# Casts tied to the first output block of tile b - 3, and transposed loads ahead of row transposes

## The chip, the cores and the metric

One core of a Trainium2 chip. The metric is the device time of one execution in microseconds (us). The kernel before takes 305.76 us, median of 3 runs (305.43 to 306.01). An execution counts as slow when it takes over 1.5% longer than the fastest of its kernel.

## The reference

Attention over 8 batches of 8 heads, 576 tokens, 64 features each, with two banded masks, followed by a two-layer network with a gate:

```python
scores = where(mask, q @ k.T / 8, -1e9)      # heads 0-3: the last 32 tokens; 4-7: every 4th of the last 128
attn   = softmax(scores) @ v
x      = attn.transpose(0, 2, 1, 3).reshape(4608, 512)
h      = x @ w_in                            # 512 -> 2048
out    = (h * sigmoid(beta * h)) @ w_out     # 2048 -> 512
```

Inputs and the output are fp32; the kernel computes in bf16 with fp32 accumulation.

## The kernel before

The 4608 tokens make 8 batches (b, 576 tokens) for the attention and 9 tiles (t, 512 tokens) for the network. Both run interleaved: while TensorE works on tile t, it also does the attention of batch b = t + 1. A small list scheduler in the kernel, the planner, decides before launch in which order every engine gets its instructions. It uses estimated durations (for a DMA, `dma` is its time in the queue and `lat` its time to land) and priorities `vt`. The planner decides **order only**. At run time the waits follow from what each instruction reads and writes.

For b >= 3 the way from inputs to the network is this. GpSimd (POOL) issues **casts**: q and k from fp32 to bf16 scratch in DRAM, v into SBUF. SyncE (SP) issues **transposed loads** dk, dq, kT, qT from the scratch. Then come the attention, the **rows** x<-xsp and x<-xdm (results to DRAM), and the **row transpose** xT<-x that brings them back transposed, for the first product of tile b - 1, b and b + 1. SyncE issues all its transfers in one order: one that must wait holds up those behind it, as dk behind xT at 95 us in the trace before (the prediction shows the lines). A small POOL copy, **pace**, stands ahead of the casts and holds them back.

```python
# the row transpose (L502 of the profile) and the rows in front of it
rows = dram_pool.tile([S // 2, HD], BF16, name=f"x{b}_{j}")
out = [plan.op([("SP", 500)], ...dma_start(out=rows[...], in_=xsp[j]...),           # L475
               [vdone[0, j], vdone[1, j]], vt_of[f"X1{j}"], dma=1200, lat=2000)]
...
o = plan.op([("SP", 1300)], lambda e: nc.sync.dma_start_transpose(out=cols, in_=rows[:]), out + dil,
            vt_of[f"X1{j}"], dma=1500, lat=3500)                                     # L502
...
def spread(e):                                       # vd<-st, L232: on POOL or VectorE, as the planner finds it
    copy(e, vd[kv][:, :, :, 0:D], vd16_of[b])
o = plan.op([("POOL", 1100), ("DVE", 620)], spread, ...)
...
def slot_h(t, fb, c0, n, vt, apart):                 # first product (L811), tanh on ACT (L820), gate on VectorE (L825)
    ...
def block_cols(t, tb, vts, lo, hi, last_one):        # second product of 128 tokens (L846), then its evacuation (result to SBUF):
    ...
    ev = plan.op([act(hi - lo), dve(hi - lo)], evac, [prev] + w, vts[3] - .01, group=g)   # osb<-bank, L861
...
def loads(b):                                        # called after tile t = b - 1 has been put on the list
    ...
    mid = (b - 2) * S + S // 2
    def t_pace(e, b=b, mid=mid):
        nc.gpsimd.tensor_copy(out=pace[:], in_=(
            xT[0:1, 0, mid - 1:mid + 1] if b - 2 >= BY_DMA else g_t[b % 2][0:1, 0, 0:2]))
    go = plan.op([("POOL", 150)], t_pace, behind + (...), b - 2.4)
    for n, (z, h0) in enumerate(((0, 4), (1, 4), (0, 0), (1, 0))):
        c = cast(b, z, h0, [go], b - 2 + .01 * n)    # L384
        ld[b]["x", z, h0] = crossbar(b, z, h0, [c] + war(*key), b - 2 + .01 * n)     # L438
```

So in the kernel before, the casts of b wait until xT of b - 2 has landed.

The softmax here doesn't subtract the row's maximum and nothing guards it: scores larger than these inputs give would overflow.

Of the kernel before, what the change touches and what calls it, by code (L numbers as in the profile page):

```python
# [8 lines left out]
FP32 = mybir.dt.float32  # L9
BF16 = mybir.dt.bfloat16  # L10
# [164 lines left out]
def kernel(  # L175
# [10 lines left out]
    nc = tc.nc  # L186
    P = 128
    B, H, S, D = q.shape
# [21 lines left out]
    DIRECT = 3  # L210
    ADDED = 1
    PAIRED = 2
    BY_DMA = 2
# [8 lines left out]
    const = lambda shape, dt, name: const_pool.tile(shape, dt, name=name)  # L222
    BANKS = [psum_pool.tile([P, 512], FP32, name=f"bank{i}") for i in range(8)]
    plan = Plan(range(8))
    E = {"ACT": nc.scalar, "DVE": nc.vector, "POOL": nc.gpsimd}

    def bank(g, dt=FP32):
        b = BANKS[g.bank][:]
        return b if dt == FP32 else b.bitcast(BF16)
# [15 lines left out]
    parity = const([P, 2], BF16, "parity")  # L245
    zero = const([P, 256], BF16, "zero")
    warm = const([P, 1], FP32, "warm")
    pace = const([1, 2], BF16, "pace")

    xT = const([P, NKT, B * S], BF16, "xT")  # L250
    g_t = [const([P, NFB, NTOK], BF16, f"g{i}") for i in range(2)]
# [139 lines left out]
    def direct_qk(b, z, h0, deps, vt):  # L391
        rows, n, dst = ((2 * GD, RD, std) if h0 else (P, RP, stp))
        src = bass.AP(tensor=(k, q)[z].tensor, offset=(k, q)[z][b, h0].offset,
                      ap=[[n * D, rows], [2 * S * D, 2], [1, n * D]])
        return load("POOL", (dst[z], src), deps, vt, 576, .41 if b else .33, lat=1100 if b else 1500)
# [25 lines left out]
    def cast(b, z, h0, deps, vt):  # L421

        dst = scratch[b, z, h0] = dram_pool.tile([S * 4 * D], BF16, name=f"s{b}_{z}_{h0}")
        src = (k, q)[z][b, h0:h0 + 4]
        if h0:
            args = [x.rearrange("(a c e) -> c a e", c=16, e=1024) for x in (dst[:], src.rearrange("h s d -> (h s d)"))]
        else:
            args = (dst[:].rearrange("(s h d) -> s h d", h=4, d=D), src.rearrange("h s d -> s h d"))
        return load("POOL", args, deps, vt, 576, .38 if h0 else .2, 500 if h0 else 1700)
# [29 lines left out]
    def war(*keys):  # L459
        return [o for key in keys for o in last.get(key, ())]  # L460

    def used(key, o):
        last.setdefault(key, []).append(o)

    def wrote(*keys):
        for key in keys:
            last[key] = []
# [3 lines left out]
    def back_dma(b, j, vt_of, vdone):  # L471

        rows = dram_pool.tile([S // 2, HD], BF16, name=f"x{b}_{j}")
        out = [plan.op(
            [("SP", 500)], lambda e: nc.sync.dma_start(  # L475
                out=rows[:, 0:HD // 2].rearrange("(i m) c -> m i c", m=QT),
                in_=xsp[j][:].rearrange("p a x h d -> p a (x h d)")),
            [vdone[0, j], vdone[1, j]], vt_of[f"X1{j}"], dma=1200, lat=2000)]
        dep = [vdone[x, rp] for x in (2, 3) for rp in range(2)]
        t0, t1 = (0, S // 2 // C) if j == 0 else (S // 2 // C, P)  # L480
        right = rows[:, HD // 2:].rearrange("(t r) c -> t r c", r=C)
        dil = [plan.op(
            [("SP", 500)], lambda e: nc.sync.dma_start(
                out=right[0:t1 - t0], in_=xdm[t0:t1].rearrange("p r x h d -> p r (x h d)")),
            dep, vt_of["X2"] if j == 0 else vt_of["X11"], dma=1100, lat=2000)]
        if j:
            dil.append(plan.op(
                [("SP", 500)], lambda e: nc.sync.dma_start(
                    out=right[t1 - t0:].rearrange("u c e -> c u e"), in_=xdt[:].rearrange("p x h d -> p (x h d)")),
                [vdone["U"]], vt_of["X11"], dma=300, lat=2000))  # L490
        for x in range(2):
            wrote(("xs", x, j))
            for o in out:
                used(("xs", x, j), o)
        if j == 0:
            wrote("xdm", "xdt")
        for o in dil[:1]:
            used("xdm", o)
        for o in dil[1:]:
            used("xdt", o)  # L500
        cols = xT[:, :, b * S + j * S // 2:b * S + (j + 1) * S // 2]
        o = plan.op([("SP", 1300)], lambda e: nc.sync.dma_start_transpose(out=cols, in_=rows[:]), out + dil,  # L502
                    vt_of[f"X1{j}"], dma=1500, lat=3500)
        xcopy.append((range(NKT), b * S + j * S // 2, b * S + (j + 1) * S // 2, o))

    def attention(b, ld, names, vts):
# [289 lines left out]


    w_in_ld, w_out_ld = {}, {}
    gop, oread = {}, {}
    count = [0, 0]  # L800

    def slot_h(t, fb, c0, n, vt, apart):
# [37 lines left out]
    def block_cols(t, tb, vts, lo, hi, last_one):  # L840
        g = Group("z" if t == NTT - 1 else "o")
        prev = None
        for part in range(4):
            def mms(e, part=part):
                for fb in range(4 * part, 4 * part + 4):
                    nc.tensor.matmul(bank(g)[:, lo:hi], lhsT=g_t[t % 2][:, fb, tb * P:(tb + 1) * P],  # L846
                                     rhs=w_out_bf[:, fb, lo:hi], start=(fb == 0), stop=(fb == NFB - 1))
            deps = [prev] + [o for fb in range(4 * part, 4 * part + 4) for o in gop[t, fb]]
            prev = plan.op([("PE", 4 * mm(hi - lo))], mms, deps + [w_out_ld[part]], vts[part],
                           acquire=g if part == 0 else None, group=g)  # L850
        oread.setdefault(t, []).append(prev)
        ob = osb[count[1] % 4]
        key = ("osb", count[1] % 4)
        count[1] += 1
        r0 = t * NTOK + tb * P
        w = war(key)
        wrote(key)

        def evac(e):
            if e == "ACT":  # L860
                nc.scalar.mul(out=ob[:, lo:hi], in_=bank(g)[:, lo:hi], mul=0.5)  # L861
            else:
                nc.vector.tensor_single_scalar(out=ob[:, lo:hi], in_=bank(g)[:, lo:hi], scalar=0.5, op=ALU.mult)
        ev = plan.op([act(hi - lo), dve(hi - lo)], evac, [prev] + w, vts[3] - .01, group=g)
        so = plan.op([("ACT" if last_one and hi == HD else "SP", 400)],
                     lambda e: (nc.scalar if e == "ACT" else nc.sync).dma_start(out=out[r0:r0 + P, lo:hi], in_=ob[:, lo:hi]),
                     [ev], vts[3], dma=.5 * (hi - lo) * 1000 / 350)
        used(key, so)



    ld = {b: {} for b in range(B)}
# [17 lines left out]
    def t_identf(e):  # L890
# [6 lines left out]
        out=beta_half[:], in_=bank(gb)[:, 0:NFB], scalar=0.5, op=ALU.mult), [bt], -1.4, group=gb)  # L897
# [7 lines left out]
    def xready(lo, hi, kts=range(NKT)):  # L905
        return [o for ks, a, b, o in xcopy if a < hi and b > lo and set(kts) & set(ks)]

    def loads(b):
        if b < DIRECT:
            base = -7.25 if b == 1 else .2  # L910
            for n, (z, h0) in enumerate(((0, 4), (1, 4), (0, 0), (1, 0))):
                ld[b]["qk", z, h0] = direct_qk(b, z, h0, war(("st", z)), base + .01 * n)
            wrote(("st", 0), ("st", 1))
            ld[b]["vd"] = direct_vd(b, war("vd16"), base + .05, war(("vt", b % 2)) + [fill4])
            wrote("vd16", ("vt", b % 2))
            ld[b]["vp"] = direct_vp(b, war(("vp", b % 2)) + [fill4], base + .06)
            wrote(("vp", b % 2))
        else:
            behind = [ld[b - 1]["x", z, h0] for z in range(2) for h0 in (0, 4)] if b > DIRECT else []

            mid = (b - 2) * S + S // 2

            def t_pace(e, b=b, mid=mid):
                nc.gpsimd.tensor_copy(out=pace[:], in_=(  # L924
                    xT[0:1, 0, mid - 1:mid + 1] if b - 2 >= BY_DMA else g_t[b % 2][0:1, 0, 0:2]))
            go = plan.op([("POOL", 150)], t_pace, behind + (
                xready(mid - 1, mid + 1) if b - 2 >= BY_DMA else gop[b - 2, 0]), b - 2.4)
            for n, (z, h0) in enumerate(((0, 4), (1, 4), (0, 0), (1, 0))):
                c = cast(b, z, h0, [go], b - 2 + .01 * n)
                key = [(((("dk", "dq") if h0 else ("kT", "qT"))[z]), b % 2, i) for i in range(2)]  # L930
                ld[b]["x", z, h0] = crossbar(b, z, h0, [c] + war(*key), b - 2 + .01 * n)
                wrote(*key)
            key = [("st", z) for z in range(2)] if b < DIRECT + 2 else [("st", b % 2)]
            ld[b]["vd"] = direct_vd(b, [go] + war(*key), b - 2 + .02, [go] + war(("vt", b % 2)))
            wrote(("st", b % 2), ("vt", b % 2))
            ld[b]["vp"] = direct_vp(b, [go] + war(("vp", b % 2)), b - 2 + .03)
            wrote(("vp", b % 2))

    steady = LATER.split()
    for t in range(NTT):  # L940
# [4 lines left out]
        b = t + 1  # L945
# [46 lines left out]
```

## Time and profile before

| | kernel before |
|---|---|
| time, median | 305.76 us |
| profiled span | 304.8 us |
| TensorE busy | 97%, at full clock in all slices |
| pace copies of b = 4, 5, 6, 7 start at | 87.0, 118.1, 148.9, 177.8 us |
| first L811 of tiles 2 to 6 starts at | 91.06, 119.86, 146.62, 177.43, 207.00 us |

The prediction below reads lines (start, duration, engine, line; "[a <-b]" is idle time before it and what ended it). Two more readings matter afterwards. The first is the page's row of the DMA engines' mean busy share, in tenths, over 40 slices of 7.6 us:

```profile
DMA  6999999999989998999699999992332100010122
```

From 8 to about 200 us the DMA engines have hardly a gap. The second is the timeline of SyncE's queue and POOL over one turn, from the pace of b = 5 to the pace of b = 6 (start, duration, engine, line; "[a <-b]" is idle time before it and what ended it):

```profile
118.12 0.30 POOL L924 COPY pace<-xT 1x2 bf16<-1x2 bf16 x1 [10.04 <-issue]
...
139.78 2.71 SPq L502 DMA_TRANSPOSE xT<-x  x1
...
143.72 1.30 SPq L502 DMA_TRANSPOSE xT<-x  x1
...
148.94 0.17 POOL L924 COPY pace<-xT 1x2 bf16<-1x2 bf16 x1 [11.41 <-DMA xT<-x]
```

The casts of b = 5 start with the first line, its four transposed loads then pass through SyncE's queue, and only behind them come the two halves of xT of b = 4. When they have landed, the next pace goes. Thus one pace leads to the next: 30.8 us for this turn.

### The profile page before, as it was taken

Reading aid. Unit: us, or ns where it says so; the run is one execution under the profiler, and the core shown is the slowest. Engines: PE = TensorE matmul, PEld = TensorE weight load, DVE = VectorE, ACT = ScalarE, POOL = GpSimd, SP = SyncE. Lnnn points to the kernel's source line nnn. Section 1 sums busy time; section 2 is a strip of 40 time slices with the busy share of each in tenths; the row PEclk is TensorE's granted clock in tenths of the full one; section 3 lists DMA queues with packets and bytes.
Section 4 is the critical chain, followed back from the end, with each engine's and each line's share of the span. In section 5 each row is a group of like instructions: output and inputs, shape, how many; then the busy total and the mean of one; then the engine's idle time right before and its main releaser. Section 6 shows DMA issues by size and latency. Waiting matters only on the chain.

```text
span 304.8 us, 6036 instructions
## 1 busy us (share of the span) xinstructions
PE 295.4 (97%) x2312; PEld 148.7 (49%) x2312; DVE 182.5 (60%) x422; ACT 171.0 (56%) x315; POOL 90.1 (30%) x132
## 2 busy tenths in 40 slices
PE   6899999999999989999999999999999999999995
PEld 5564545554544444444444444444444444444454
DVE  3468965888866745875677567757764434343300
ACT  2767963877547644755565556556554454554411
POOL 8978662746055104600470065100000000000000
PEclk9999999999999999999999999999999999999999
DMA  6999999999989998999699999992332100010122
GB/s 102 172 210 202 206 184 208 180 142 167 204 193 193 149 152 170 197 137 237 134 180 177 158 202 173 173 231 58 95 92 73 39 34 34 34 37 34 50 88 71
DMA packets 117376, 42.47 MB, mean 139 GB/s; under 512 B 93748, under 2 KB 110916, under 8 KB 117348
## 3 DMA queue, kind: packets, MB, share of 16 engines
q0 software_dynamic: 66672, 19.66, 64.9%
q1 hardware_dynamic: 50532, 22.36, 37.1%
q8 instruction: 18, 0.29, 0.4%
q14 instruction: 10, 0.08, 0.1%
q10 hardware_dynamic: 144, 0.07, 0.1%
HBM read 39.32 MB, written 18.87 MB: 191 GB/s over the span
## 4 chain that ended last, share of the span: by engine, by line
PE 74%; DMA 16%; POOL 3%; SPq 2%; DVE 2%; issue 1%; ACT 0%; POOLq 0%; DVEq 0%
PE bank L846 36%; PE bank L811 32%; DMA vd<-in_v_dram 4%; DMA st<-in_q_dram 4%; DMA dq<-s 3%; DMA w_in_bf<-in_moe_w_in_dram 3%; DMA x<-xsp 2%; DVE g L825 2%; SPq L438 2%; PE bank L673 1%; PE bank L729 1%; PE bank L639 1%; PE bank L714 1%; POOL st L384 1%; POOL vp L384 1%
## 5 line engine op out<-in xcount | busy, mean ns | idle before, releaser
L846 PE MATMUL bank<-w_out_bf,g 128*128 128x512 bf16 (+2 forms) x608 | 143.3, 368 | 0.0
L825 DVE SCALAR_TENSOR_TENSOR g<-tnh,bank 128x512 bf16<-128x512 bf16 x144 | 97.7, 685 | 74.4 <-ACT tnh L820 73.7
L811 PE MATMUL bank<-xT,w_in_bf 128*128 128x512 bf16 (+1 forms) x584 | 141.2, 376 | 0.3 <-DMA w_in_bf<-in_moe_w_in_dram 0.3
L820 ACT ACTIVATE tnh<-bank,beta_half 128x512 bf16<-128x512 f32 x144 | 98.5, 689 | 74.4 <-PE bank L811 73.3
L811 PEld LDWEIGHTS <-w_in_bf 128*128 128x128 bf16 x584 | 54.7, 98 | 60.4 <-DMA w_in_bf<-in_moe_w_in_dram 0.4
L846 PEld LDWEIGHTS <-g 128*128 128x128 bf16 x608 | 54.6, 98 | 55.7
L861 ACT ACTIVATE osb<-bank 128x512 f32<-128x512 f32 (+1 forms) x36 | 21.2, 589 | 32.0 <-PE bank L846 31.8
L576 ACT ACTIVATE pt<-bank 128x288 bf16<-128x288 f32 x64 | 21.5, 418 | 5.5 <-PE bank L673 5.4
L576 ACT ACTIVATE ptd<-bank 128x512 bf16<-128x512 f32 x32 | 16.9, 603 | 6.5 <-PE bank L639 6.5
L596 DVE TENSOR_TENSOR xsp<-bank,rcp 96x384 bf16<-96x384 f32 x32 | 17.7, 554 | 1.1
L384 POOL DMA_DIRECT2D vp<-in_v_dram x10 | 17.7, 1776 | 0.5 <-PE bank L455 0.5
L595 DVE RECIPROCAL rcp<-bank 128x4 f32<-128x4 f32 (+2 forms) x72 | 12.9, 180 | 6.3 <-PE bank L729 4.8
L580 DVE TENSOR_TENSOR ptd<-ptd,mask_d 128x512 bf16<-128x512 bf16 x27 | 11.9, 452 | 5.6 <-ACT ptd L576 4.5
L924 POOL COPY pace<-xT 1x2 bf16<-1x2 bf16 x4 | 0.8, 207 | 47.1 <-DMA xT<-x 37.1
L596 DVE TENSOR_TENSOR xdm<-bank,rcp 128x256 bf16<-128x256 f32 x32 | 13.6, 425 | 1.1
L384 POOL DMA_DIRECT2D vt<-in_v_dram x16 | 13.5, 1020 | 0.0
L384 POOL DMA_DIRECT2D s<-in_q_dram x10 | 13.5, 1347 | 0.0
L729 PEld LDWEIGHTS <-pt 128*128 128x128 bf16 x192 | 9.4, 97 | 5.9
L384 POOL DMA_DIRECT2D s<-in_k_dram x10 | 11.2, 1121 | 1.1 <-issue 1.1
L232 POOL COPY dkt<-dk 128x384 bf16<-128x384 bf16 x7 | 3.8, 544 | 22.8 <-DMA dk<-s 17.4
L729 PE MATMUL bank<-vp,pt 128*128 128x65 bf16 x192 | 10.4, 193 | 0.0
L714 PEld LDWEIGHTS <-ptd 128*128 128x128 bf16 x128 | 6.7, 98 | 4.7 <-issue 0.2
(108 smaller groups left out, 177.2 us busy)
## 6 DMA issues: line engine op xcount, KB each, us to landing
out_dram<-osb SPq DMA_DIRECT2D x35, 256.0 KB, 2.7
s<-in_k_dram POOLq DMA_DIRECT2D x10, 288.0 KB, 7.0
s<-in_q_dram POOLq DMA_DIRECT2D x10, 288.0 KB, 10.3
vp<-in_v_dram POOLq DMA_DIRECT2D x7, 384.0 KB, 18.2
w_out_bf<-in_moe_w_out_dram POOLq DMA_DIRECT2D x2, 1024.0 KB, 16.3
st<-in_k_dram POOLq DMA_DIRECT2D x6, 288.0 KB, 13.8
st<-in_q_dram POOLq DMA_DIRECT2D x6, 288.0 KB, 12.7
x<-xsp SPq DMA_DIRECT2D x12, 144.0 KB, 7.3
```

The costliest lines, as they stand in the source:

```text
L384: {"POOL": nc.gpsimd, "SP": nc.sync}[queue].dma_start(out=out, in_=in_)
L576: nc.scalar.activation(out=w(), in_=sc(), func=ACT.Exp, scale=SCALE)
L580: E[e].tensor_tensor(out=w(), in0=w(), in1=m(), op=ALU.mult)
L595: nc.vector.reciprocal(out=r, in_=p[..., D])
L596: nc.vector.tensor_tensor(out=dst, in0=p[..., 0:D], in1=r.unsqueeze(len(p.shape) - 1).to_broadcast(list(p.shape[:-1]) + [D]), op=ALU.mult)
L714: nc.tensor.matmul(pv[:, r, a], lhsT=ptd[:, x - 2, j, 2 * r + a], rhs=vd[kv][:, 2 * (x - 2) + a, 2 * r + j, 0:D + 1], start=True, stop=True)
L729: nc.tensor.matmul(pv[:, a, h2, :], lhsT=pt[x][:, (3 * j + a) * 2 + h2], rhs=vp[kv][:, (2 * x + h2) * NI + 3 * j + a, 0:D + 1], start=True ...
L811: nc.tensor.matmul(bank(g)[:, a:z], lhsT=w_in_bf[:, kt, fb * P:(fb + 1) * P], rhs=xT[:, kt, xo + a:xo + z], start=(i == 0 and kt == kts[0] ...
L820: nc.scalar.activation(out=th[:, 0:n], in_=bank(g)[:, 0:n], func=ACT.Tanh, scale=beta_half[:, fb:fb + 1])
L825: nc.vector.scalar_tensor_tensor(out=g_t[t % 2][:, fb, c0:c0 + n], in0=th[:, 0:n], scalar=1.0, in1=bank(g)[:, 0:n], op0=ALU.add, op1=ALU.mult)
L846: nc.tensor.matmul(bank(g)[:, lo:hi], lhsT=g_t[t % 2][:, fb, tb * P:(tb + 1) * P], rhs=w_out_bf[:, fb, lo:hi], start=(fb == 0), stop=(fb = ...
L861: nc.scalar.mul(out=ob[:, lo:hi], in_=bank(g)[:, lo:hi], mul=0.5)
```

## The change

Intent: start the casts on TensorE's own progress (the evacuation of the first output block of tile b - 3) instead of on the arrival of xT of b - 2, and tell the planner that rows and row transposes land sooner, so that it places transposed loads ahead of row transposes on SyncE.

```diff
-    pace = const([1, 2], BF16, "pace")
+    pace = const([1, 1], FP32, "pace")
...
-            [vdone[0, j], vdone[1, j]], vt_of[f"X1{j}"], dma=1200, lat=2000)]
+            [vdone[0, j], vdone[1, j]], vt_of[f"X1{j}"], dma=900, lat=1300)]
...
-                dep, vt_of["X2"] if j == 0 else vt_of["X11"], dma=1100, lat=2000)]
+                dep, vt_of["X2"] if j == 0 else vt_of["X11"], dma=900, lat=1300)]
...
-                [vdone["U"]], vt_of["X11"], dma=300, lat=2000))
+                [vdone["U"]], vt_of["X11"], dma=300, lat=1300))
...
-                    vt_of[f"X1{j}"], dma=1500, lat=3500)
+                    vt_of[f"X1{j}"], dma=1400, lat=2200)
...
+        evac_of[t, tb] = ev, ob, key
...
-            behind = [ld[b - 1]["x", z, h0] for z in range(2) for h0 in (0, 4)] if b > DIRECT else []
-            mid = (b - 2) * S + S // 2
-            def t_pace(e, b=b, mid=mid):
-                nc.gpsimd.tensor_copy(out=pace[:], in_=(
-                    xT[0:1, 0, mid - 1:mid + 1] if b - 2 >= BY_DMA else g_t[b % 2][0:1, 0, 0:2]))
-            go = plan.op([("POOL", 150)], t_pace, behind + (
-                xready(mid - 1, mid + 1) if b - 2 >= BY_DMA else gop[b - 2, 0]), b - 2.4)
+            ev, ob, key = evac_of[b - 3, 0] if b > DIRECT else (gop[b - 2, 0][-1], None, None)
+            def t_pace(e, b=b, ob=ob):
+                nc.gpsimd.tensor_copy(out=pace[:], in_=g_t[b % 2][0:1, 0, 0:1] if ob is None else ob[0:1, 0:1])
+            go = plan.op([("POOL", 150)], t_pace, [ev], b - 2.4)
+            if key:
+                used(key, go)
```

## The prediction

> **What bounds the kernel now.** I read the page first, then the matmuls by form, the waits, the timeline of TensorE, and last the chain of waits with the timelines of the other queues.
>
> ```profile
> PE 295.4 (97%) x2312; PEld 148.7 (49%) x2312; DVE 182.5 (60%) x422; ACT 171.0 (56%) x315; POOL 90.1 (30%) x132
> ...
> PEclk9999999999999999999999999999999999999999
> ```
>
> TensorE is busy 97% of 304.8 us at the full clock. Busy alone could hide starvation, since records of pipelined matmuls overlap, so I checked the rate:
>
> ```profile
> 95.81 5.78 PE L811 MATMUL bank<-xT,w_in_bf 128*128 128x512 bf16 x26
> ...
> 106.78 2.75 PE L846 MATMUL bank<-w_out_bf,g 128*128 128x512 bf16 x12
> 110.72 0.62 PE L639 MATMUL bank<-dq,dk 64*128 64x128 bf16 x16 [1.19 <-DMA dq<-s]
> ...
> 116.71 0.43 PE L673 MATMUL bank<-qT,kT 64*128 64x96 bf16 x12
> ```
>
> 26 matmuls of 512 columns span 5.78 us; less the 0.38 us that one record lasts, 25 spacings take 5.40 us, 216 ns each. The stretches of 10 us from 240 to 290 us hold 48 each: also full rate. So TensorE itself is the bound, and only its stalls can be removed. Up to about 60 us there are several, at the start, but the order of instructions is the same in both kernels until about 88 us. After that the timeline has exactly one marked stall: 1.19 us ahead of the dilated scores of b = 4 (L639), waiting for dq; by starts, the twelfth L846 begins at 106.78 + 11 x 0.216 = 109.16 and L639 1.56 us later; less its own 0.216 and the 0.095 that a change to 64-row matmuls costs everywhere, 1.25 us are lost. A second one is too short to be marked: the four matmuls of L846 at 115.75 should give way at 116.62, but L673 starts at 116.71 and the start-to-start distance is 0.16 us too long (it waits for qT). **1.4 us of 305.8, 0.5%, is all that this change can win.** Where the long one comes from:
>
> ```profile
> 88.18 6.87 DMA x<-xsp
> ...
> 95.09 1.79 SPq L502
> ...
> 97.07 4.55 SPq L438
> ...
> 101.67 8.92 DMA dq<-s
> ...
> 110.72 0.62 PE bank L639 x16
> ```
>
> The SyncE queue is in order. The row transpose xT of b = 3 (L502) stood at its head from 92.2 us on, waiting for its rows (x<-xsp, issued 88.18, landed 95.06); behind it dk and dq (L438). The casts had been held up earlier:
>
> ```profile
> 82.50 0.60 ACT L861 ACTIVATE osb<-bank 128x512 f32<-128x512 f32 x1 [1.95 <-PE bank L846]
> ...
> 86.99 0.18 POOL L924 COPY pace<-xT 1x2 bf16<-1x2 bf16 x1 [10.97 <-DMA xT<-x]
> 87.48 0.61 POOL L384 DMA_DIRECT2D s<-in_k_dram  x1 [0.31 <-issue]
> ...
> 89.71 1.33 POOL L384 DMA_DIRECT2D st<-in_v_dram  x1
> ...
> 102.02 1.04 POOL L232 COPY vd<-st 128x1024 bf16<-128x1024 bf16 x1 [6.59 <-DMA st<-in_v_dram]
> ```
>
> The pace copy waited for xT of b = 2. The reader should also note the output block's copy at 82.50: that is the new trigger for b = 4.
>
> **What the Trainium skill says.** "DMA: Bandwidth & Descriptors", section "Issuing engines are not separate DMA queues": DMAs of all issuing engines run on the same 16 DMA engines and interleave. The trace agrees: the same cast of v took 12.3 us to its reader for b = 4 (89.71 to 102.02), beside row writes, and 7.3 us for b = 6. Casts issued earlier are therefore not free. "Perfetto Trace Analysis", section "DMA Instruction — HWDGE (DVE, Sync)": a profiled issue begins once its semaphores are satisfied, so a wait shows only as a hole in SyncE's timeline; here 92.2 to 95.09. "TensorE: Matmul & The Clock Gate", section "Back-to-back issue gap", gives about 216 ns for an isolated 512-column matmul and 131 ns sustained; this trace gives 216 sustained, and the trace decides. "TensorEngine Tiling (Array Packing)", section "Key Properties", says that a change of tiling mode drains the array: here some 95 ns more between two starts, at each entry to and exit from the 64-row scores; both kernels make the same number of such changes, so it cancels.
>
> **The change, part by part.** (1) The pace copy reads one fp32 word of osb instead of two words of xT: 0.2 us on POOL either way, off the path. It no longer waits for the previous transposes or for xT. For b = 4: osb is done at 83.1, so the casts start at about 83.7 instead of 87.5, 3.8 us earlier. For b = 5 to 7 it also depends on where TensorE now stands.
>
> (2) The planner's figures for landing are lower, so it believes xT to be early, and orders everything anew. The order shows the same 2312 matmuls of the same sizes, so TensorE's work is unchanged to the nanosecond. What moves is when xT is needed. Summing each matmul in front at 216 ns for 512 columns and in proportion below, the first L811 of each tile comes earlier by the work that now stands behind it, and by the 1.4 us once that is gone: tile 2 from 91.06 to 88.3 us, tile 3 from 119.86 to 114.1 (4.3 of work and 1.4), tile 4 from 146.62 to 139.0, tile 5 from 177.43 to 172.7, tile 6 from 207.00 to 204.5.
>
> (3) On SyncE, dk, dq and kT of b = 4 now precede xT of b = 3. dk is ready at 83.7 + 4.5 to 7 = 88 to 91 us, dq about 93; dq landed 8.9 us after its issue before, so about 102, while L639 would run at 108.5. **The 1.25 us go**, and the 0.16 of qT too (L673 now comes later).
>
> (4) The price: xT of b = 3. Tile 3, tokens 1536 to 2047, needs both halves of b = 3 (tokens 1728 to 2303). From dk at 90 us: dk 2.3, dq 3.6, kT 3.7, xT 1.8, an output 0.5 (issue times of the later tiles) gives 102; qT waits for its cast (issued 88, 11.7 to 13.9 us as in the later tiles) and ends near 104.5; only then x<-xsp of the second half, landing 4.6 to 5.8 us later, 110; xT 1.8 more and 2.1 to 3.9 to land: **114 to 116.5, against a need at 114.1. Estimated stall 1 us**, 0 to 2.4.
>
> (5) The copy vd of b = 4 moves from POOL to VectorE, behind the gate of the fifth L811 group of tile 2, at about 95.1 us. Its v is cast at 85.9 and lands 7.3 to 12.3 us later: 93.2 to 98.2. VectorE is in order, so the gates behind it stand too, and TensorE, with some 2 us of banks in hand, stalls 0 to 2.7 us, estimated 0.5. This delay and that of (4) overlap: a later TensorE needs xT later.
>
> (6) Tile 5 needs the first half of b = 5. Casts of b = 6 follow the first block of tile 3, whose last matmuls move back by 3.6 us of work: they start at about 149 us plus the stalls so far, against 149.4; qT's cast lands 16 us later and qT issues for 2.5 to 5.1; then an output, x<-xsp, now ahead, and xT: landing 173 to 176 against a need at 172.7 plus the stalls. Estimated 0.5 more. Tiles 4 and 6 come out with about 1 us in hand.
>
> Sum: 305.76 - 1.4 + (1 and 0.5 overlapping to 1.0) + 0.5 = **305.8 us**.
>
> **The rivals.** *A, clean win:* transfers go faster when the casts are out of the way earlier, no new stall: 304.3. For it: 1.5 us of margin at most is missing anywhere in (4) to (6), and the new landing figures look as if fitted to measurements. Against: the needs are 2.5 to 7.6 us earlier, with the DMA row of the page at 9 tenths in most slices up to 200 us. *B, the wait is moved:* stalls at tile 3 and again at tile 5, with the casts of the next tile tied to TensorE's own progress so that nothing is caught up: 306.5 to 308.5. For it: (4) and (6). *C, pile-up:* casts at 83.7 meet the xT transposes of b = 2 (issued 81.77 to 84.47, landed 86.95; need 88.3), and VectorE blocks behind the vd copy: 307 to 311. For it: 12.3 us for v under such load. Against: before, xT of b = 2 landed 1.3 us ahead of the new need. *D, faster by over 2%,* would need 6.1 us of stalls to remove; 1.4 exist.
>
> **Range and chances.** A has 40%, B 40%, C 20%, some at the mild end. That makes 304.1 to 308.3 for 8 in 10, the floor at 304.3 less run-to-run scatter of 0.3. Slower by over 2% (311.9) needs C at its worst: 4%. Faster by over 2%: 1%.
>
> **What the profile after would show.** Right: the marked wait of L639 on dq gone; pace copies at about 83 us; 2312 matmuls at 216 ns as before; new waits, if any, of L811 on xT near 114 and 173 us, or of TensorE near 97 us with VectorE waiting for st. Wrong: a stall at any other place; a changed start before 88 us; a sum of stalls after 88 us above 4 us; or a dq wait that survives.

## The result, and the profile after

The changed kernel takes **327.3 us** (median of 4 runs, 324.92 to 328.42), the kernel before 305.85 us in the same rounds. The ratio is 1.069, 95% interval 1.063 to 1.076: slower by 21.5 us. The prediction was 305.8, with 304.1 to 308.3 as its range; it was wrong. (Ratios here and below are the mean time of one kernel's fast runs over that of the other's of the same rounds, so not quite the ratio of the medians quoted.)

The page after, rows of TensorE, clock and DMA:

```profile
PE 300.1 (93%) x2275; PEld 150.2 (46%) x2312; DVE 181.1 (56%) x418; ACT 171.0 (53%) x315; POOL 91.3 (28%) x136
...
PEclk9999999999998999998997999999999999999999
DMA  6999999999799929996299967999233111000022
```

The work is the same: 2312 weight loads (37 records of matmuls are missing from this trace), and the busy share of the DMA row times the span gives about 192 us before and 194 us after. But the DMA row now has **holes** (a 2 at 113 to 121 us, a 2 at 153 to 161 us, a 6 at about 190 us), so for several microseconds at a time there was little to transfer, and the clock row has dips.

The waits after (engine, line, what was waited for: us in total, times, longest):

```profile
DVE vd L232 <- DMA st<-in_v_dram: 11.8, 3, 4.8
...
PEld L811 <- DMA xT<-x: 6.0, 3, 2.9
...
PE bank L811 <- DMA xT<-x: 4.3, 2, 2.4
...
PE bank L811 <- DVE g L825: 3.7, 1, 3.7
```

The wait of L639 for dq is gone, as intended. In its place are waits of L811 for xT and for a gate that stood behind VectorE's vd copy. The chain of waits after, in order of time (start, length, what):

```profile
85.88 14.89 DMA st<-in_v_dram
...
100.86 0.19 DVE vd L232
...
102.54 3.72 PE bank L811 x9
...
107.77 2.59 PE bank L811 x12
...
136.11 8.74 DMA x<-xsp
144.93 3.88 DMA xT<-x
...
148.85 0.39 PE bank L811
...
157.81 0.61 ACT osb L861
...
158.47 0.18 POOL pace L923
...
160.97 12.09 DMA st<-in_v_dram
173.07 0.43 DVE vd L232
```

Read it downwards. The cast of v for b = 4 takes 14.9 us; VectorE stands until it is there, and TensorE behind it until 102.54. Nine matmuls then take 3.72 us, some 0.41 us each, about half speed, while the twelve from 107.77 on run at 0.216. At 136.11 come rows and row transpose; tile 4 can start only at 148.85. Then the line that decides: **the evacuation at 157.81, which releases the pace and so the casts of b = 6, comes 9 us after tile 4's first L811**, because TensorE's order now has them that way round. So a late xT delays the next casts, these delay the next v and the next xT, and so on.

TensorE's stalls after 88 us, from its timeline (time lost beyond the 216 ns rate):

| start, us | lost, us | waits for | slow clock afterwards costs, us |
|---|---|---|---|
| 88.5 | 1.1 | tile 2: xT of b = 2 | |
| 98.6 | 3.9 | gate behind vd of b = 4 | 1.6 |
| 146.2 | 2.6 | tile 4: xT of b = 4 | 1.7 |
| 171.4 | 2.9 | gate and mask product behind vd of b = 6 | 1.6 |
| 208.0 | 1.0 | mask product behind vd of b = 7 | |
| 222.0 | 2.1 | tile 6: xT of b = 6 | |

The sum is 18.5; less the 1.4 of stalls that the change removes, 17.1 of the 18.2 us between the two profiled spans (323.0 and 304.8). Two losses too small for the table are most of the rest: 0.4 us ahead of tile 5 at 188.3 (its xT landed at 188.7) and 0.4 in the attention's matmuls at 209. This profiled execution is the quickest of its kernel's four.

The pace copies show the same thing in one row each:

| pace copy of b = | 4 | 5 | 6 | 7 | from 4 to 7 |
|---|---|---|---|---|---|
| before | 87.0 | 118.1 | 148.9 | 177.8 | 90.8 |
| after | 83.4 | 120.9 | 158.5 | 195.1 | 111.7 |

The first is 3.6 us earlier (3.8 predicted). But a turn takes 37 us instead of 30, 20.9 us more in three turns. Not all of that is waiting: in the new order, counted as below, the matmuls from the first paced block to the last add up to 96.1 us, and the stalls and slow clock of the table up to 195 us, with the 0.4 at 188.3, to 15.8.

Where the turn comes from can be counted in TensorE's order, without any times: add up each matmul's columns at 216 ns per 512 in the order that the planner makes. (For the first three rows the trace before, less its stalls, has 31.2, 32.0 and 30.8 us between the same instructions.)

| work between | before | after |
|---|---|---|
| end of block (2,0), which paces b = 5, and first L811 of tile 4, which needs xT of b = 4 | 31.2 us | 26.2 us |
| the same, block (3,0) and tile 5 | 32.1 us | 26.4 us |
| the same, block (4,0) and tile 6 | 30.9 us | 26.5 us |
| end of block (3,0) relative to first L811 of tile 4 | 1.2 us ahead | 7.2 us behind |

The pace copy comes 0.9 us after the block's last matmul (120.88 against 119.97 for b = 5), so that much goes off. The trace after has the way from the pace through casts, transposed loads, rows and row transposes to xT; its lines for the pace copies are

```profile
120.88 0.18 POOL L923 COPY pace<-osb 1x1 f32<-1x1 f32 x1 [16.18 <-ACT osb L861]
...
158.47 0.18 POOL L923 COPY pace<-osb 1x1 f32<-1x1 f32 x1 [1.73 <-ACT osb L861]
...
195.08 0.18 POOL L923 COPY pace<-osb 1x1 f32<-1x1 f32 x1 [15.32 <-ACT osb L861]
```

and the last semaphore events of the row transposes that tiles 4, 5 and 6 need give the landings:

| changed kernel, turn of b = | 5 | 6 | 7 |
|---|---|---|---|
| xT landed at, us | 148.80 | 188.69 | 224.00 |
| the way, from the pace copy, us | 27.9 | 30.2 | 28.9 |
| what the order leaves after the pace copy, us | 25.3 | 25.5 | 25.6 |
| short by, us | 2.6 | 4.7 | 3.3 |
| TensorE's stalls and slow clock in that stretch, us | 2.6 | 4.9 | 3.5 |

So the order leaves less time than the way takes, and that in every turn; what is short is what TensorE loses, whether it waits for xT itself or first for the v of the same late casts. In the old order there are 4 to 6 us more.

### The profile page after: what moved, and what is told of

It is laid out like the page before. It is cut to its first block, busy times and chain, and to the rows that moved or that the text cites. A ratio compares the mean times of both kernels' runs of the same rounds, so it can differ in the third digit from the quotient of the medians.

```text
span 323.0 us, 5999 instructions
## 1 busy us (share of the span) xinstructions
PE 300.1 (93%) x2275; PEld 150.2 (46%) x2312; DVE 181.1 (56%) x418; ACT 171.0 (53%) x315; POOL 91.3 (28%) x136
## 4 chain that ended last, share of the span: by engine, by line
PE 56%; DMA 31%; POOL 6%; issue 2%; DVE 2%; ACT 1%; SPq 1%; POOLq 0%; ACTq 0%; DVEq 0%
PE bank L846 26%; PE bank L811 26%; DMA st<-in_v_dram 8%; DMA s<-in_q_dram 5%; DMA w_in_bf<-in_moe_w_in_dram 4%; DMA vd<-in_v_dram 4%; DMA st<-in_q_dram 4%; DMA xT<-x 3%; DMA x<-xsp 3%; POOL s L384 2%; POOL st L384 1%; PE bank L729 1%; PE bank L639 1%; DVE g L825 1%; POOL vp L384 1%
## 5 line engine op out<-in xcount | busy, mean ns | idle before, releaser
L811 PE MATMUL bank<-xT,w_in_bf 128*128 128x512 bf16 (+1 forms) x561 | 144.3, 383 | 10.9 <-DMA xT<-x 4.3
L846 PE MATMUL bank<-w_out_bf,g 128*128 128x512 bf16 (+2 forms) x594 | 142.9, 370 | 1.3 <-issue 0.6
L811 PEld LDWEIGHTS <-w_in_bf 128*128 128x128 bf16 x584 | 54.6, 99 | 70.8 <-issue 8.9
L846 PEld LDWEIGHTS <-g 128*128 128x128 bf16 x608 | 55.3, 98 | 57.7 <-issue 1.6
L861 ACT ACTIVATE osb<-bank 128x512 f32<-128x512 f32 (+1 forms) x36 | 21.2, 588 | 27.8 <-PE bank L846 25.2
L923 POOL COPY pace<-osb 1x1 f32<-1x1 f32 x4 | 0.7, 178 | 40.4 <-ACT osb L861 40.4
```

Source lines behind the costliest of these rows:

```text
L811: nc.tensor.matmul(bank(g)[:, a:z], lhsT=w_in_bf[:, kt, fb * P:(fb + 1) * P], rhs=xT[:, kt, xo + a:xo + z], start=(i == 0 and kt == kts[0] ...
L846: nc.tensor.matmul(bank(g)[:, lo:hi], lhsT=g_t[t % 2][:, fb, tb * P:(tb + 1) * P], rhs=w_out_bf[:, fb, lo:hi], start=(fb == 0), stop=(fb = ...
L861: nc.scalar.mul(out=ob[:, lo:hi], in_=bank(g)[:, lo:hi], mul=0.5)
```

## The experiments

Because the waits follow from what an instruction reads, the trigger can be exchanged **without** the planner knowing: if only the source of the pace copy is edited, all five engines keep their order. This separates the two halves of the change. Line numbers in edited kernels can be a few higher (L812 to L814 are then the first product). All runs gave correct results.

### 1. Old order, new trigger

```diff
-                nc.gpsimd.tensor_copy(out=pace[:], in_=( xT[0:1, 0, mid - 1:mid + 1] if ... ))
+                nc.gpsimd.tensor_copy(out=pace[:], in_=g_t[...] if ob is None else ob[0:1, 0:1])
```
(in the kernel before; the planner's dependencies are left as they were)

> Every engine's order is that of the kernel before; only what the pace copy reads is new (osb of the first block of tile b - 3). Theory 1, the new order is what costs (VectorE's vd copy above all): no new stall, the dq wait of 1.25 us shrinks because the casts of b = 4 start at 83.6 instead of 87.5; 304.5 to 306.5 us. Rival, the trigger is what costs (casts that wait for TensorE's progress, so that delays feed on themselves, and that meet the xT transposes): over 312 us, stalls of TensorE on xT.

Measured: 305.19 us (304.90 to 309.46, 4 runs), before 305.60; ratio 1.002 (0.995 to 1.009). **The trigger alone costs nothing that stands out of the noise.** Three runs took 304.9 to 305.3 us; the profiled one took 309.46. Its timeline of TensorE shows why:

```profile
93.82 4.54 PE L811 MATMUL bank<-xT,w_in_bf 128*128 128x512 bf16 x13 [2.40 <-DMA xT<-x]
```

Tile 2 waited 2.4 us for xT of b = 2, which shared the DMA engines with the casts released at 83.35, and a slow clock followed. So rival C's meeting of casts and xT happens in this trace, and it is not repeated later. Whether the new trigger makes such an execution more frequent is not shown: in the rounds of runs 9 to 11 one of eight executions of the kernel before took 310.17.

The same trace shows why the old order bears the new trigger. The way from the pace copies of b = 5, 6 and 7 (119.20, 149.21, 180.01) to the xT that is needed (landed 147.01, 178.01, 209.21) takes 27.8, 28.8 and 29.2 us, as long as in the changed kernel. But this order leaves 30.3, 31.2 and 30.0 us (the table's work less 0.9), and the tiles don't wait.

### 2. New order, old trigger

```diff
-                nc.gpsimd.tensor_copy(out=pace[:], in_=g_t[...] if ob is None else ob[0:1, 0:1])
+                nc.gpsimd.tensor_copy(out=pace[:], in_=( xT[0:1, 0, mid - 1:mid + 1] if ... ))
```
(in the changed kernel)

> Every engine's order is that of the changed kernel; only the pace copy reads xT again. Theory 1, order: still over 318 us, with VectorE's vd copies waiting for st by 3 us or more and TensorE behind them. Rival, trigger: falls to 306 to 311 us.

Measured: 314.03 us (312.94 to 316.13); ratio 1.028 (1.024 to 1.033). The order alone costs 8 us: stalls of 4.1 us at 97 (vd), 1.5 at 145.6, 0.9 at 168 and 1.7 at 181.5. With run 1 this makes a square:

| | casts wait for xT | casts wait for the output block |
|---|---|---|
| order before | 305.85 | 305.19 |
| order after | 314.03 | 327.3 |

The two halves cost 0 and 8 us alone and 21.5 us together: about 13 us belong to neither half but to their **combination**. In the same order the pace copies of b = 5, 6 and 7 stand at 117.7, 153.5 and 185.9 us in run 2, and at 120.9, 158.5 and 195.1 with the new trigger: later by 3, 5 and 9 us.

### 3. The changed kernel with every vd copy on POOL

```diff
         def spread(e):
+            e = "POOL" if b >= DIRECT else e
             copy(e, vd[kv][:, :, :, 0:D], vd16_of[b])
```

> The changed kernel, with the vd copies of b = 4, 6, 7 on POOL at the same places in the program; nothing else moves. Theory 1 as told from the trace after: the three stalls behind vd go, 3.9 + 2.9 + 1.0 us, and with them the slow matmuls after the first two, 1.9 + 1.4; 311 to 318 us, and the waits of L811 on xT remain, perhaps smaller. Rival, transfers that come too late for this order whoever waits for them: the same bytes are needed a moment later by the scores or xT, and the time stays over 321 us.

Measured: 323.36 us, median of four; one of them (330.81) was slow, the three fast ones took 321.07 to 323.52. Ratio of the fast ones 1.055 (1.051 to 1.060). My first theory, that VectorE standing behind v was the main cost, **fell**: removing it gives back 4 us of 21.5, not most of it. The stalls moved to xT; two of the five, from the timeline of TensorE:

```profile
145.94 1.04 PE L812 MATMUL bank<-xT,w_in_bf 128*128 128x512 bf16 x4 [2.77 <-DMA xT<-x]
...
185.26 4.06 PE L812 MATMUL bank<-xT,w_in_bf 128*128 128x512 bf16 x12 [4.21 <-DMA xT<-x]
```

A tile that was held up by vd in the changed kernel is held up by xT here. Both are ends of the same late casts.

### 4. Both edits: new order, casts wait for xT, vd on POOL

```diff
+            e = "POOL" if b >= DIRECT else e
...
-                nc.gpsimd.tensor_copy(out=pace[:], in_=g_t[...] if ob is None else ob[0:1, 0:1])
+                nc.gpsimd.tensor_copy(out=pace[:], in_=( xT[0:1, 0, mid - 1:mid + 1] if ... ))
```

> Order of the changed kernel, pace on xT as before, vd copies on POOL as before. If vd on VectorE and the trigger are the whole cost: 304 to 307 us. If the order of SyncE and TensorE itself costs (dk, dq, kT ahead of xT, needs of xT 3 to 8 us earlier): over 310 us, with TensorE waiting for xT at tiles 3 to 6.

Measured: 315.16 us (313.82 to 316.16); ratio 1.031 (1.027 to 1.035). With the old trigger, vd on POOL gains nothing at all (314.03 without it). Against run 3, the trigger alone makes 8.0 us (323.19, the middle one of its fast runs, and 315.16), with the same order and no vd in VectorE's way.

### 5. New order, casts for b >= 5 released earlier, by the last gate of tile b - 3

```diff
-    xT[0:1, 0, mid - 1:mid + 1] if b > DIRECT else ...
+    g_t[(b - 3) % 2][0:1, NFB - 1, 0:2] if b > DIRECT + 1 else xT[0:1, 0, mid - 1:mid + 1] if b > DIRECT else ...
```
(on top of run 4) It was to open the loop.

> Order of the changed kernel on every engine, vd on POOL; pace of b = 4 on xT as before, pace of b = 5 to 7 on the last gate of tile b - 3, which stands ahead of the first L811 of tile b - 2 on TensorE. Theory 2, a closed loop: pace, 25 us of transfers, xT, first L811 of the next tile, some 9 us of matmuls, the end of the first output block, pace; a round of 37 us where TensorE needs 31. This trigger stands outside the loop, so the waits on xT of tiles 4 to 6 go and only tile 3 waits (4 to 6 us with its slow matmuls): 306 to 311 us. Rival, the 16 DMA engines cannot do a batch in less than some 31 us and merely become busier: as the same order with pace on xT, 313 to 316 us.

Measured: 325.54 us, median of four; two of them (326.02 and 330.59) were slow, the fast ones took 320.74 and 325.06. Ratio of these 1.056 (1.048 to 1.065). **A miss.** The casts of b = 5, released at 107.7, met the rows and the row transpose of b = 3: the second row write took 7.7 us to land where the changed kernel has 4.1, the row transpose behind it 8.2 where it has 3.5. From the timeline of TensorE:

```profile
124.84 1.01 PE L812 MATMUL bank<-xT,w_in_bf 128*128 128x512 bf16 x2 [11.12 <-DMA xT<-x]
```

So casts can also come too early. And the loop was not opened after all: the pace of b = 6, whose gate was long done, ran at 158.2 us, since POOL is in order and a mask of b = 5 stood ahead of it. The run tells nothing for or against the loop, but it shows that early casts aren't safe.

### 6. New trigger with the old figures (the planner knows the trigger)

The diff of the change without its `dma` and `lat` figures; against the changed kernel:

```diff
-            [vdone[0, j], vdone[1, j]], vt_of[f"X1{j}"], dma=900, lat=1300)]
+            [vdone[0, j], vdone[1, j]], vt_of[f"X1{j}"], dma=1200, lat=2000)]
...
-                    vt_of[f"X1{j}"], dma=1400, lat=2200)
+                    vt_of[f"X1{j}"], dma=1500, lat=3500)
```

> The pace part of the change alone, ordered anew by the planner with the old landing figures. First L811 of tiles 3, 4, 5, 6 is needed 0, 5, 1 and -1 us earlier than before (by counting matmuls), and only at tile 4 does it stand ahead of the end of the block that triggers. Theory 2: one turn of the loop, some waiting at tile 2 (casts meeting xT) and at tile 4 or 5; 306 to 312 us. Rival, the trigger costs by itself: over 315 us.

Measured: 311.77 us (307.58 to 314.64). Two of the four runs were slow; the two fast ones took 307.58 and 309.83, and no interval can be given, so whether it is over 2% stays unclear. The planner's order here leaves 27.0 us of work for b = 5 and 28.4 for b = 6, but 32.1 for b = 7; the stalls (3.0 us at 118, 0.6 at 142.6, 0.7 at 163, 0.6 at 179) are milder than in the changed kernel.

### 7. New figures with the old trigger (the planner knows it)

The diff of the change without the part in `loads`; against the kernel before:

```diff
-            [vdone[0, j], vdone[1, j]], vt_of[f"X1{j}"], dma=1200, lat=2000)]
+            [vdone[0, j], vdone[1, j]], vt_of[f"X1{j}"], dma=900, lat=1300)]
...
-                    vt_of[f"X1{j}"], dma=1500, lat=3500)
+                    vt_of[f"X1{j}"], dma=1400, lat=2200)
```

> The landing figures of the change alone, pace on xT. First L811 of tiles 3, 4, 5, 6 is needed 3, 5, 5 and 4 us earlier than before. Theory 2: waits on xT at several tiles, as the transfers keep their 31 us round; 309 to 315 us. Rival, the figures are harmless and only their coming together with the trigger costs: 304.5 to 307 us.

Measured: 311.77 us (310.02 to 313.54); ratio 1.020 (1.015 to 1.025), at the edge of 2%. Stalls: 2.7 us at 105.7 (a gate), 1.4 at 142.6, 0.9 at 174.6, the last two for xT. The figures alone make the planner place tile 4's first L811 5.1 us of work earlier (131.1 against 136.2), and the kernel pays 6 us.

### 8. The kernel before with one other figure

An attempt to gain the 1.4 us of the old stalls: the transposed loads are said to land later, so that the planner puts the scores behind them later.

```diff
-                       deps, vt, dma=288 * 1024 / .2 / 1000, lat=4000)
+                       deps, vt, dma=288 * 1024 / .2 / 1000, lat=7000)
```

> An attempt to beat the kernel before: its transposed loads of k and q get a landing figure of 7 us in place of 4 (they took 9 to 11 us in the trace), nothing else. L639 of b = 4 then stands 3.5 us of work later. If the planner's figures decide by where they put the needs: the dq wait of 1.25 us goes, 304.0 to 305.5 us; a new wait on xT at tile 4 (needed 2 us earlier) could eat it.

Measured: 309.38 us (308.82 to 310.09); ratio 1.012 (1.010 to 1.015). It is slower: tile 4's first L811 again moved forward by 2.1 us of work and now waits 2.4 us for xT; dq (0.6 us at 112.5) still waits. Two more stalls, 1.1 us each, stand at 119 (qT of b = 4) and 121 (tile 3, xT). The sensitive quantity is again where the first L811 of a tile stands.

### 9. and 10. A delay in the way, in both orders

If the way from pace to pace is a loop that TensorE waits on, a delay in it must add up turn by turn, less the margin. Three POOL copies of 1 x 1600, together 4.64 us in the trace, stand between the arrival of xT and the pace of b = 5, 6 and 7. Casts are released by xT in both.

```diff
+                for _ in range(3 if b > DIRECT + 1 else 0):
+                    nc.gpsimd.tensor_copy(out=late[:, 0:1600], in_=late[:, 0:1600])
```

On the kernel before:

> The kernel before with the casts of b = 5, 6 and 7 held back by about 5 us each: three copies of 1600 elements on one partition of POOL between xT and the pace copy; nothing else moves. Theory 2b, the way from pace to xT (some 25 us) and back to the next pace is a loop that in the kernel before takes just TensorE's 31 us, so a delay adds up over its turns: 5 + 5 + 5 less 1.4 to 3 us of margin, 316 to 319 us. No loop, only a margin: the largest single delay counts once, 308 to 310 us. Rival, what costs in the changed kernel is casts that come early and meet other transfers: later casts do no harm, 304 to 307 us.

On run 4:

> The same delay of 5 us in the changed order with pace on xT and vd on POOL (315.2 us without the delay). Theory 2b: no margin is left, so 3 x 5 more, 327 to 331 us, which would be what the osb trigger did in this order. No loop: 319 to 321 us. Rival of early casts: 311 to 315 us.

Measured: 314.89 us (313.39 to 315.76) for the order before, +9.6 us on 305.25 (ratio 1.030, 1.027 to 1.034); 328.41 us (327.15 to 328.72) for the order after, +13.2 us on run 4's 315.16 (ratio to the kernel before 1.075, 1.073 to 1.078). Three delays are 13.9 us. In the new order **nearly all of it arrives in the time**: no margin. In the old order 4.3 us are swallowed and the rest arrives: a loop with some margin. The timelines of TensorE, order before (first fence) and order after (second):

```profile
172.52 1.02 PE L813 MATMUL bank<-xT,w_in_bf 128*128 128x512 bf16 x4 [1.52 <-DVE g L827]
206.39 1.86 PE L813 MATMUL bank<-xT,w_in_bf 128*128 128x512 bf16 x4 [2.90 <-DVE g L827]
```

```profile
117.68 1.01 PE L814 MATMUL bank<-xT,w_in_bf 128*128 128x512 bf16 x2 [3.63 <-DMA xT<-x]
149.19 0.61 PE L814 MATMUL bank<-xT,w_in_bf 128*128 128x512 bf16 x1 [4.83 <-DMA xT<-x]
189.43 4.26 PE L814 MATMUL bank<-xT,w_in_bf 128*128 128x512 bf16 x11 [4.04 <-DMA xT<-x]
226.17 4.45 PE L814 MATMUL bank<-xT,w_in_bf 128*128 128x512 bf16 x11 [3.27 <-DMA xT<-x]
```

In the first, the stalls behind late transfers come only late (the gates of these two lines stood behind a VectorE copy that waited for dq); in the second, every tile from 3 to 6 pays 3 to 5 us. Rival B's picture, one or two waits that have moved, allows neither.

The delay had a side effect in the old order that was not intended:

```profile
116.82 4.65 POOL L929 COPY late<-late 1x1600 bf16<-1x1600 bf16 x3
...
120.12 0.33 PE L731 MATMUL bank<-vp,pt 128*128 128x65 bf16 x5 [1.12 <-DVE pt L582]
```

While the three copies ran, three products of VectorE (pt, L582) took 1.0, 1.6 and 1.6 us where the others take 0.3, and TensorE lost 1.9 us behind them (1.3 ahead of this L731, 0.6 ahead of the L813 at 122.61). By this one trace, about 7.7 of the 9.6 us went through the loop, and about 6 were swallowed. In the trace of the new order no VectorE instruction is drawn out so. Also, both runs release the casts by xT: they show the loop from pace through xT to pace, not the way round through the output block. For that one stands the table of turns above.

### 11. Run 3 with the casts of b = 4 back on xT

```diff
-    ob[0:1, 0:1] if b > DIRECT else ...
+    ob[0:1, 0:2] if b > DIRECT + 1 else xT[0:1, 0, mid - 1:mid + 1] if b > DIRECT else ...
```

> The changed kernel with vd on POOL (323.4 us) and the pace of b = 4 alone back on xT, so that the casts of b = 4 do not meet the xT transposes of b = 2. If that meeting is a large part: TensorE's wait at tile 2 (3.4 us in the trace of that kernel) goes, 316 to 320 us. If the loop of b = 5 to 7 is what counts: tile 3 waits instead, as it does with pace on xT, and the time stays at 320 to 325 us.

Measured: 322.93 us (319.86 to 324.32); ratio 1.057 (1.050 to 1.063). The stall at tile 2 is gone, but the time is that of run 3 within its scatter: tiles 3 to 6 then wait 2.2, 2.2, 4.6 and 3.2 us. So the first meeting of casts and xT at 84 us (rival C) is not what costs; the turns of b = 5 to 7 are.

## Why the prediction was wrong, point by point

**The bound, right.** TensorE at 216 ns, 1.4 us of stalls to win. The change did win them.

**(1) to (3), right.** Pace at 83.4 (predicted about 83.7 for the casts, measured 83.64); the dq wait gone; and the places where xT is needed were right: the no-stall need of tile 4 was given as 139.0, the losses ahead of it add up to 6.6 us, and the stall began at 146.2. (A slip in the bound's working: the four matmuls of L846 start at 115.59 in the line shown, not at 115.75; the 0.16 us for qT is right.)

**(4), wrong place.** Tile 3 was to wait 1 us for xT of b = 3. It didn't wait: TensorE had already lost 7 us by then. The prediction's own sentence "a later TensorE needs xT later" held here.

**(5), the mechanism right, the size off.** "TensorE ... stalls 0 to 2.7 us, estimated 0.5". Measured 3.9, since v took 14.9 us where I had allowed 7.3 to 12.3 from the trace before. On top came 1.6 us at about half clock, a term that the sum did not have at all; after the three longer stalls it made 4.9 us together. Run 3 shows that, even so, VectorE's place in the way is worth only 4 us of the whole.

**(6), the step that failed.** "They start at about 149 us plus the stalls so far" was right but for a slip in its working: the last matmuls of tile 3's first block move back by 2.5 us of work, not 3.6, which makes it about 147.6. With the 10.9 us of stalls and slow clock up to there that is 158.5; the casts began at 158.7. But from it I concluded "Estimated 0.5 more. Tiles 4 and 6 come out with about 1 us in hand." I added the stalls so far to the need (172.7) and left the landing (173 to 176) without them, so that a stall would buy time for the next tile. It does for a transfer already under way (tile 3). It doesn't where the next casts are themselves released by TensorE's progress **behind** the stall: then need and supply shift together, and every turn pays its own shortfall again. The way was also taken too short, 24 to 27 us (149 to 173 or 176); the trace before has 26.6, 27.8 and 28.4 us from the pace copies of b = 5, 6 and 7 to the xT that is needed, and the trace after 27.9, 30.2 and 28.9, where the order allows 25.3 to 25.6. I had all three needed numbers (the block's place, the need, the way's length) and never subtracted within one turn. Tile 4 lost 2.6 us and tile 6 lost 2.1, with 1 us "in hand" predicted for each; in the turn between, the late v cost 2.9.

**The rivals.** B named it ("nothing is caught up") but was sized as two waits, 306.5 to 308.5. C's parts were both seen (1.1 us at tile 2; VectorE behind vd) and it had the highest ceiling, 311; but by runs 3 and 11 they aren't the main part. The chances came out at 95% for within 2% because a kernel that hardly stalls does not show in its profile how little margin its loop has. An added delay, as in run 9, does show it, if it is checked for side effects.

**What stays open.** No run removed the loop in the new order while keeping everything else (run 5 tried and collided), so its share is known through the exchanged trigger and through the account of the turns in one trace, and by added delay for the loop with the old trigger, not through its removal. How much of the way's 28 us is transfers slowing each other was not separated. And no version beat the kernel before: run 1's three quick runs are 0.3 to 0.7 us below its median, inside the scatter, with one run of four 4 us above.

## What to carry to other kernels

When a prefetch is released by the consumer's progress, write down one turn: from the release through the transfers to the consumer's need, and ask whether the next release stands ahead of that need in the consumer's own order or behind it. Behind it, any shortfall is paid in every turn; ahead of it, once. A change of trigger and a change of order may each be harmless and still not be harmless together, so try them in a square; and if a pipeline shows no stall, add a known delay to see how much margin it has.

## What the Trainium skill lacked or had wrong

- "TensorE: Matmul & The Clock Gate", section "Back-to-back issue gap": gives 131 ns sustained for a 512-column matmul. Here it is 216 ns throughout, as in twelve in 2.59 us.
- The same page, section "Part 1: The HAM clock gate", has the clock fall to half after an idle window of about 3.4 us that runs freely. These traces agree on the window: the clock records show half speed for 3.41 us or a whole multiple of it, and in the trace after it begins at 102.44, 150.22 and 174.12, 14 and 7 windows apart. But the window need not be idle. Between 60 and 240 us of all thirteen traces, each fall to half clock follows a window in which TensorE was busy for at most 42% of the time, and no window at full clock with 43% or more was followed by one. So a stall of 2.52 us could bring half speed, and one of 3.4 us (run 3), spread over two windows at 57% and 49%, did not. The cost, 1.6 to 1.7 us after each of the three longer stalls in the changed kernel, is no small one beside the stall itself.
- "DMA: Bandwidth & Descriptors" gives fixed costs, and for the HBM access alone a latency under load; I found no time for a whole transfer beside others. The same cast of v took 7.3 and 12.3 us before, 14.9 and 12.1 after, and a row write 8.7 us.
- No page treats a prefetch loop and its margin: here 4.3 us of 13.9 added delay were swallowed in one order (about 6 without the side effect on VectorE), and about 0.7 us in the other.
